# Strassen block products for the last four feed-forward blocks of an attention and gated feed-forward kernel, in a second pass of 768 tokens

## Chip, core and metric

One core of a Trainium2 chip runs the whole program. The metric is device time in microseconds, the median of several executions. Times inside an execution are from the hardware profiler: us from the first instruction.

## The reference

Eight batches of eight heads, 576 tokens, head size 64. Attention is linear: queries and keys are projected to 128 features, shifted by their largest magnitude, and taken through exp of plus and minus. The result goes through a gated feed-forward layer of 4608 tokens, model size 512, inner size 1536:

```python
def _moe_ref(x, w_gate, w_val, w_out):
    gate = 1.0 / (1.0 + np.exp(-(x @ w_gate)))
    val = x @ w_val
    return (gate * val @ w_out).astype(np.float32)
# x: attention output, (4608, 512); w_gate, w_val: (512, 1536); w_out: (1536, 512)
```

All inputs and outputs are float32.

## The kernel before

*The feed-forward layer.* Tokens are cut into 9 chunks of 512 (`CW`, `NCH`), the inner size into 12 blocks of 128 (`NJ`), the model size into 4 slices of 128. x lies feature-major: a tile is 128 features x 512 tokens. To keep float32 accuracy with one-pass matmuls, each operand is kept as two `float32r` halves, high (`xh`, `wh`, `hh`) and low (`xl`, `wl`, `hl`), and a product is three matmuls: high by high, high by low, low by high. For a chunk and a block, `gate` runs 4 slices x 3 matmuls for the gate and as many for the value, each with its own 128x128 weights and 512 moving columns. ScalarE takes tanh and exp of the gate; VectorE clears a sign bit, makes two combined steps with the value, and after ScalarE's rounding (`hh`) subtracts to get `hl`. `mm_out` multiplies the halves by the output weights: 3 matmuls of 512 columns for each of 4 token tiles.

*Stages.* While attention runs, `first_js` takes blocks 0 to 3 of every chunk whose x is ready, and stores half sums in `yscr`. After attention its memory is given to the second stage (`swap`): for each chunk C, blocks 4 to 11 (`js`) accumulate in four PSUM banks, and VectorE adds the stored y and sends the result out. Weights of blocks 4 to 7 lie in `vh`, `vl`, those of 8 to 11 take the place of blocks 0 to 3 in `wh`, `wl`. Each chunk's x is loaded twice for this stage: `zh`, `zl` for blocks 4 to 7, `xh`, `xl` for 8 to 11. `weigh` unpacks one 512-column weight piece of the float64-like input words into its halves.

*Order.* The program is not run as written. Each step is put into a plan (`pe`, `dve`, `on_act`, `sp`) with an assumed duration, a rank, and the buffers it reads and writes. `Plan.run` then lays all steps out: at each engine it starts, among steps that could start about first, the one of lowest rank. A step that needs a buffer of a ring takes the slot that is free earliest. Each engine runs its steps in that fixed order; semaphores do the waiting. The assumed cost of a VectorE step is 0.07 us plus 1/960 us an element, of a ScalarE step 0.08 plus 1/1200.

*PSUM.* Five banks are the ring `r_a` (named bank in the profile), three are `r_g` (gate).

Of the kernel before, what the change touches and what calls it, by code (L numbers as in the profile page):

```python
# [8 lines left out]
F32 = mybir.dt.float32  # L9
# [24 lines left out]
JA = 4  # L34
JR = 8
NQ = 3
# [9 lines left out]
XN = 4  # L46
HN = 5
FSTEP = 4.5
KOFF = 20.0
NOFF = 40.0  # L50


class Slot:
    def __init__(self, make):
        self.make, self.made, self.free, self.taken = make, None, 0.0, False

    def tile(self):
        if self.made is None:
            self.made = self.make()
        return self.made  # L60


class Buf:
# [6 lines left out]
    def __call__(self):  # L70
        if self.ap is None:
            x, n = self.slot.tile(), 1
# [20 lines left out]
class Plan:  # L93
# [29 lines left out]
    def run(self):  # L123
# [7 lines left out]
        def pick(b, taken):  # L131
            best = None
            for ring in b.rings:
                for s in ring:
                    if not s.taken and s not in taken and (best is None or s.free < best.free):
                        best = s
            return best

        def start(o):
            t = max(o.ready, free[o.eng])  # L140
            if o.eng == "PE" and mode not in (None, o.mode[0]):
                t = max(o.ready, free[o.eng] + self.SWITCH)
            taken = []
            for b in o.bufs:
                if b.rings and b.slot is None:
                    s = pick(b, taken)
                    if s is None:
                        return None
                    taken.append(s)
                    t = max(t, s.free)  # L150
            return t

        order, left = [], len(self.ops)
        while left:
# [19 lines left out]
            for b in o.bufs:  # L174
                if b.rings and b.slot is None:
                    b.slot = pick(b, ())
                    b.slot.taken = True
            free[o.eng] = t + o.busy
# [5 lines left out]
            if o.eng == "PE":  # L184
                mode = o.mode[-1]
            for slot in o.opens:
                slot.free, slot.taken = end, False
            for b in o.bufs:
                b.left -= 1
                b.end = max(b.end, end)  # L190
                if not b.left and b.slot:
                    b.slot.free, b.slot.taken = b.end, False
            for n in o.then:
# [14 lines left out]
def attention_moe(  # L208
# [21 lines left out]
    def ring(where, tag, n, width, dtype=F32):  # L230
        def make(i):
            pool = stage[where] if isinstance(where, str) else where
            return pool.tile([P, width], dtype, tag=f"{tag}{i}", name=f"{tag}{i}")

        return [Slot(lambda i=i: make(i)) for i in range(n)]

# [15 lines left out]
    xscr = [dram.tile([P, NC4, CW], F32, tag=f"xs{c}", name=f"xs{c}") for c in range(NCH)]  # L252
    yscr = [dram.tile([4, P, DM], F32, tag=f"ys{c}", name=f"ys{c}") for c in range(NCH)]
    dens = [dram.tile([2, S], F32, tag=f"den{i}", name=f"den{i}") for i in range(B * NP)]

    r_a = ring(ps, "bank", BANKS, DM)
    r_g = ring(ps, "gate", 8 - BANKS, DM)
    r_wh, r_wl = (ring(ff, f"w{a}", JA, 3 * DM, F32R) for a in "hl")
    r_xh, r_xl = (ring(ff, f"x{a}", XN, CW, F32R) for a in "hl")
    r_hh, r_hl = (ring(ff, f"h{a}", HN, CW, F32R) for a in "hl")  # L260
    r_u, r_t = (ring(ff, a, 2, CW) for a in "ut")
    r_y = ring(ff, "y", 2, DM)
    r_raw = ring(ff, "wraw", 2, 2 * DM, U32)
    r_mid = ring(ff, "wmid", 2, 2 * DM, U32) if RAW < 3 * JA else []
    r_top = ring(ff, "wtop", 2, DM, U32)
    r_wh2, r_wl2 = (ring("two", f"v{a}", JR - JA, 3 * DM, F32R) for a in "hl")
    r_xh2, r_xl2 = (ring("two", f"z{a}", NC4, CW, F32R) for a in "hl")
    r_hh2, r_hl2 = (ring("two", f"k{a}", 3, CW, F32R) for a in "hl")
    r_y1 = ring("two", "y1", 4, DM)
    at_rings = {}  # L270
# [13 lines left out]

    def dve(n, fn, reads, writes, rank, k=1.0):
        return plan.op("DVE", 0.07 + n / 960 / k, 0.16, fn, reads, writes, rank)

# [18 lines left out]
    ymark = [Buf() for _ in range(NCH)]  # L306
    closing = []

# [370 lines left out]

    def weigh(j, m, r, deep, rings):  # L680
        if m == 0:
            weights[j] = [(Buf([rings[0]], [P, 3 * DM]), Buf([rings[1]], [P, 3 * DM])), []]
        (wh, wl), _ = weights[j]
        ms = slice(m * DM, m * DM + DM)
        raw = Buf([r_raw], [P, 2 * DM])
# [5 lines left out]
        def hi():  # L691
# [3 lines left out]
            512 << 10,  # L695
            lambda: nc.sync.dma_start(raw(), w_moe[j, :, m, :].bitcast(U32)), [], [raw], r,
        )
        dve(
# [8 lines left out]
        if deep:  # L707
# [24 lines left out]
        on_act(  # L732
            DM, lambda: act.copy(wh()[:, ms], top().bitcast(F32)), [top], [(wh, m)], r,
        )
# [9 lines left out]
        else:  # L744
# [29 lines left out]
            ),  # L774
            [src], [(wl, m)], r,
        )

    def load_x(c, r, rings, after=()):
# [109 lines left out]
    for i in range(N):  # L888
        since = len(plan.ops)
        attend(i)  # L890
        closing += plan.ops[since:]
        if i < 4:
            for m in range(3):
                weigh(i, m, WAT + WSTEP * (3 * i + m), 3 * i + m >= RAW, (r_wh, r_wl))
        if i % NP == NP - 1:
            lo = 0 if i < NP else ((i // NP) * S) // CW
            for c in range(lo, ((i // NP + 1) * S) // CW):
                r = due(i + 1) + LEAD + 66.0 * (c - lo)
                if c:
                    load_x(c, r - 20.0, [(r_xh, r_xl)])  # L900
                first_js(c, r, FSTEP)

    def swap():
# [3 lines left out]
    last = plan.op("X", 0.0, 0.0, swap, after=closing)  # L907
    last.opens = [s for r in (r_wh2, r_wl2, r_xh2, r_xl2, r_hh2, r_hl2, r_y1) for s in r]
    for s in last.opens:
        s.taken = True  # L910

    base = due(N) + 60.0
    for j in range(JA, NJ):
        rings = (r_wh2, r_wl2) if j < JR else (r_wh, r_wl)
        for m in range(3):
            weigh(j, m, base + 10.0 * (j - JA) + 3 * m, False, rings)

    late = None
    js = list(range(JA, NJ))
    accs = {}  # L920
    for C in range(NCH):
        load_x(NCH + C, base + 150.0 + 100.0 * C, [(r_xh2, r_xl2)], [last])
        load_x(2 * NCH + C, base + 200.0 + 100.0 * C, [(r_xh, r_xl)], [last])
        for i, j in enumerate(js):
            r = base + 200.0 + 100.0 * C + 10.0 * i
            near = j < JR
            hs = gate(
                NCH + C if near else 2 * NCH + C, j, r, [r_g, r_a], False,
                (r_hh2, r_hl2) if near else (r_hh, r_hl),
            )  # L930

            def step(C=C, i=i, j=j, hs=hs, r=r):
                if i == 0:
                    accs[C] = [Buf([r_a], [P, DM]) for _ in range(4)]
                for t in range(4):
                    acc = accs[C][t]
                    pe(
                        "f", 0.685,
                        lambda acc=acc, t=t: mm_out(acc, t, hs, j, i == 0, i == len(js) - 1),
                        [*hs] + [(x, 2) for x in weights[j][0]], [acc], r + 13.0, 0.3,  # L940
                    )
                    if i == len(js) - 1:
                        y1, y = Buf([r_y1], [P, DM]), Buf([r_y], [P, DM])
                        sp(
                            256 << 10,
                            lambda t=t, y1=y1: nc.sync.dma_start(y1(), yscr[C][t]),
                            [(ymark[C], t)], [y1], r - 20.0, [last],
                        )
                        dve(
                            DM,  # L950
                            lambda y=y, y1=y1, acc=acc: vec.scalar_tensor_tensor(
                                y(), acc(), 0.5, y1(), op0=ALU.mult, op1=ALU.add
                            ),
                            [acc, y1], [y], -90.0,
                        )
                        sp(
                            256 << 10,
                            lambda t=t, y=y: nc.sync.dma_start(
                                out[C * CW + t * P : C * CW + t * P + P, :], y()
                            ),  # L960
                            [y], [], r,
                        )

            step()
    order = plan.run()
# [60 lines left out]
```

## Time and profile before

| | before |
|---|---|
| median of 3 executions | 1203.58 us (1202.52 to 1206.42) |
| the profiled execution | 1204.94 us, span 1203.0 us |
| TensorE (PE) busy | 1185.0 us, 99% |
| weight loads (PEld) | 914.8 us |
| VectorE (DVE) busy | 778.1 us |
| ScalarE (ACT) busy | 556.4 us |
| bytes moved by DMA | 129.04 MB |

A row of a group of instructions reads: source line, engine, operation, written tile <- read tiles, shapes, how many; then busy time and mean duration in ns, then idle time of the engine just before them and what ended it. A row of the timeline reads: start in us, length in us, engine, line, operation. A weight load is a LDWEIGHTS of engine PEld; it stands beside the matmuls of PE. L809 is the gate and value matmul, L857 the output matmul, L951 the final sum, L438 and L333 are projections of attention.

### The profile page before, as it was taken

To read this page: it belongs to the slowest core of one execution; us is meant where nothing else is said; L and a number is where in the kernel's file an instruction comes from. 1 tells how busy PE (TensorE), PEld (TensorE's weight loads), DVE (VectorE), ACT (ScalarE), POOL (GpSimd) and SP (SyncE) were. 2 spreads that over 40 slices of the span, in tenths; PEclk is the share of its full clock that TensorE was granted. 3 is DMA by queue.
4 is the path that set the end of the run, shared out by engine and by line. 5 is a ranking of instruction groups with operands and counts; after the bars stand their busy time and mean duration, and the time that the engine had idled before them with its cause. 6 is when DMAs were issued, how large, how long until landed. Compare 5 with 4: busy or idle time off the path is not lost.

```text
span 1203.0 us, 21037 instructions
## 1 busy us (share of the span) xinstructions
PE 1185.0 (99%) x8508; PEld 914.8 (76%) x8508; DVE 778.1 (65%) x1489; ACT 556.4 (46%) x1054; POOL 0.7 (0%) x6
## 2 busy tenths in 40 slices
PE   8999999999999999999999999999999999999998
PEld 6666567667776767778888888888888888888886
DVE  6999998887888888579849744344343444343433
ACT  6867776566666575545545422222222222222211
POOL 0000000000000000000000000000000000000000
PEclk9999999999999999999999999999999999999999
DMA  6763552534434441355334413121130213131300
GB/s 229 224 212 116 167 175 88 165 115 137 119 125 133 118 156 53 100 178 164 108 106 140 140 36 105 35 81 61 35 106 24 84 33 105 36 105 36 102 4 35
DMA packets 72936, 129.04 MB, mean 107 GB/s; under 512 B 16904, under 2 KB 23176, under 8 KB 72840
## 3 DMA queue, kind: packets, MB, share of 16 engines
q1 hardware_dynamic: 72840, 127.71, 33.5%
q8 instruction: 66, 1.08, 0.4%
q14 instruction: 30, 0.25, 0.1%
HBM read 99.09 MB, written 28.45 MB: 106 GB/s over the span
## 4 chain that ended last, share of the span: by engine, by line
PE 86%; DVE 6%; DMA 5%; ACT 1%; issue 1%; SPq 0%; DVEq 0%
PE gate L809 35%; PE bank L857 18%; PE bank L809 11%; PE gate L857 6%; PE bank L522 4%; PE bank L564 3%; PE bank L333 2%; DMA rb<-den 2%; PE bank L582 2%; PE bank L438 1%; DMA den<-dn 1%; PE bank L536 1%; PE bank L548 1%; DVE d L488 1%; DMA wraw<-w_moe 1%
## 5 line engine op out<-in xcount | busy, mean ns | idle before, releaser
L809 PE MATMUL gate<-xh,wh 128*128 128x512 f32 x464 | 183.5, 396 | 0.6 <-ACT u L829 0.6
L809 PE MATMUL gate<-xl,wh 128*128 128x512 f32 x464 | 180.9, 390 | 0.6 <-DVE xl L662 0.6
L809 PE MATMUL gate<-xh,wl 128*128 128x512 f32 x464 | 180.9, 390 | 0.0
L833 DVE TENSOR_SCALAR t<-t 128x512 uint32<-128x512 uint32 x108 | 45.6, 423 | 171.4 <-ACT t L828 171.3
L828 ACT ACTIVATE t<-gate 128x512 f32<-128x512 f32 x99 | 59.0, 596 | 189.0 <-PE gate L809 188.8
L846 ACT CAST hh<-u 128x512 fp32r<-128x512 f32 x72 | 44.7, 621 | 166.1 <-DVE u L843 166.0
L380 ACT ACTIVATE ek<-ek 128x512 f32<-128x512 f32 (+1 forms) x192 | 96.6, 526 | 28.4 <-DVE ek L368 27.1
L809 PEld LDWEIGHTS gate<-xh,wh 128*128 128x128 f32 x464 | 87.1, 188 | 20.4 <-issue 1.2
L809 PEld LDWEIGHTS gate<-xh,wl 128*128 128x128 f32 x464 | 87.1, 188 | 18.8
L809 PEld LDWEIGHTS gate<-xl,wh 128*128 128x128 f32 x464 | 87.2, 188 | 18.5 <-DVE xl L662 1.0
L809 PE MATMUL gate<-zl,vh 128*128 128x512 f32 x208 | 81.0, 389 | 0.0
L809 PE MATMUL gate<-zh,vl 128*128 128x512 f32 x208 | 81.0, 389 | 0.0
L809 PE MATMUL gate<-zh,vh 128*128 128x512 f32 x208 | 80.9, 389 | 0.0
L838 DVE SCALAR_TENSOR_TENSOR t<-t,gate 128x512 f32<-128x512 f32 x69 | 47.3, 685 | 51.9 <-PE gate L809 51.3
L843 DVE SCALAR_TENSOR_TENSOR u<-u,t 128x512 f32<-128x512 f32 x108 | 74.5, 690 | 7.6 <-DVE t L838 0.5
L522 PE MATMUL bank<-ek,vin 128*32 128x256 f32 x1240 | 73.3, 381 | 4.9 <-ACT d L446 4.0
L846 ACT CAST kh<-u 128x512 fp32r<-128x512 f32 x36 | 22.4, 621 | 117.6 <-DVE u L843 117.6
L522 PEld LDWEIGHTS bank<-ek,vin 128*32 128x32 f32 x1240 | 37.7, 110 | 46.0 <-issue 11.0
L848 DVE TENSOR_TENSOR hl<-u,hh 128x512 fp32r<-128x512 f32 x72 | 49.6, 689 | 30.9 <-ACT hh L846 30.9
L857 PE MATMUL bank<-wh,hl 128*128 128x512 f32 x168 | 65.6, 390 | 0.0
L857 PE MATMUL bank<-wh,hh 128*128 128x512 f32 x168 | 65.6, 390 | 0.0
L857 PE MATMUL bank<-wl,hh 128*128 128x512 f32 x168 | 65.3, 389 | 0.0
(176 smaller groups left out, 2475.5 us busy)
## 6 DMA issues: line engine op xcount, KB each, us to landing
wraw<-w_moe SPq DMA_DIRECT2D x36, 512.0 KB
xl<-xs SPq DMA_DIRECT2D x68, 256.0 KB
kin<-k SPq DMA_DIRECT2D x32, 320.0 KB
qin<-q SPq DMA_DIRECT2D x32, 320.0 KB
vin<-v SPq DMA_DIRECT2D x32, 320.0 KB
ys<-y SPq DMA_DIRECT2D x36, 256.0 KB
zl<-xs SPq DMA_DIRECT2D x36, 256.0 KB
y<-ys SPq DMA_DIRECT2D x36, 256.0 KB
```

The lines of the kernel that those rows point to most:

```text
L333: nc.tensor.matmul(pk[hd]()[:, t, :], x()[head(hd), t * P : t * P + P], wk[head(hd), :], start=True, stop=True,)
L380: lambda g=g, sg=sg: act.activation(ek[g]()[:, :, sg * F : sg * F + F], ek[g]()[:, :, F:], AF.Exp, scale=1.0 - 2.0 * sg,),
L522: nc.tensor.matmul(o_[o : o + Q, : 2 * F], vx()[:, 2 * t + hd, o % D : o % D + Q], (e0, e1)[hd][:, t, :] if t < 4 else e2[:, 0, :], start= ...
L564: nc.tensor.matmul(nm()[o : o + Q, :], w()[:, sg, o : o + Q], es[sg]()[:, o // D, cs], start=sg == 0, stop=sg == 1, tile_position=(0, o),)
L809: nc.tensor.matmul(o(), a()[:, ws], x(), start=cc + n == 0, stop=cc == NC4 - 1 and n == 2,)
L828: on_act(CW, lambda: act.activation(t(), g(), AF.Tanh, scale=0.5), [g], [t], z)
L833: vec.tensor_scalar(tu, tu, 0x7FFFFFFF, None, op0=ALU.bitwise_and)
L838: lambda: vec.scalar_tensor_tensor(t(), t(), 1.0, vl(), op0=ALU.add, op1=ALU.mult),
L843: lambda: vec.scalar_tensor_tensor(u(), u(), 1.0, t(), op0=ALU.min, op1=ALU.mult),
L846: on_act(CW, lambda: act.copy(hh(), u()), [u], [hh], z)
L848: CW, lambda: vec.tensor_tensor(hl(), u(), hh().bitcast(F32), op=ALU.subtract),
L857: nc.tensor.matmul(acc(), a()[:, ts], w()[:, ws], start=first and i == 0, stop=last and i == 2)
```

## The change

Blocks 8 to 11 leave the second stage and are done in a pass of their own after it. The second stage (pass 1 below) now takes blocks 4 to 7 alone (`JB = 8`) and stores its sums in `y2scr`. Pass 2 goes over 6 blocks of 768 tokens (`DC`), each two halves of 384 (`HT`). A pair of inner blocks by the model size's two halves makes a 2 by 2 grid of weight blocks, 256 x 128 each; x makes a 2 by 2 grid of 256 features x 384 tokens. Their product is made of seven block products in place of eight (Winograd's form of Strassen's scheme). One block product is 2 slices x 3 matmuls of 384 columns.

- `combine` builds, for each of 2 pairs and for gate and value, the seven weight operands in halves, in pass 1; `keep_out` stages the output weights in memory (`wscr`).
- `x_blocks` loads x for one block of tokens, makes T1 to T4 with four subtractions and splits seven operands.
- `group` runs the seven products in four PSUM banks of `r_a`. Three banks are written twice; VectorE adds in between and after.
- `gated` and `valued` are the former gate steps in pieces of 384. Output parts accumulate in `r_g`; `finish` adds the stored sum and sends it out.
- All rings of the feed-forward layer become ranges of a few large tiles (`arena`), so that the passes can use the same memory differently; a slot is free when all of its cells are. `turn` opens pass 2's loads once pass 1's loads and staged weights are through.

The core of the diff, and the new functions:

```diff
-    base = due(N) + 60.0
-    for j in range(JA, NJ):
-        rings = (r_wh2, r_wl2) if j < JR else (r_wh, r_wl)
...
+    for j in range(JA, JB):
+        weigh_all(j, base + 10.0 * (j - JA), 3, lambda m: False, (r_wh2, r_wl2))
...
+    def combine(n, m, r):
...
+        for i in range(2):
+            weigh(JB + 2 * n + i, m, r + 3 * i, False, gh, gl, ...)
+            dve(DM, ...)       # w = gh + gl
+        for o, a, b, op, reads in (
+            (0, (w, 2), (w, 3), ALU.add, [(w, 1)]),
+            (1, (x, 0), (w, 0), ALU.subtract, [(w, 0)]),
+            (2, (w, 1), (x, 1), ALU.subtract, [(w, 0)]),
+            (3, (w, 0), (w, 2), ALU.subtract, [w]),
+        ):
+            dve(KH, ...)
+        for n_, o, i in ((3, 4, 0), (1, 2, 3)):
+            on_act(n_ * KH, ...)   # high halves
+            dve(n_ * KH, ...)      # low halves
...
+    js = list(range(JA, JB))
+    for C in range(NCH):
+        load_x(NCH + C, r0 - 20.0, [(r_zh2, r_zl2) if C > 1 else (r_zh, r_zl)], ...)
...
+    turn = plan.op("X", 0.0, 0.0, lambda: None, after=loads + staged)
...
+    def x_blocks(dc, r):
...
+        fetch(b11, 0, 0)
+        fetch(tmp[0], 0, 1)
+        fetch(b22, 1, 1)
+        fetch(b21, 1, 0)
+        less(tmp[1], tmp[0], b11)
+        split("11", b11)
+        less(tmp[2], b22, tmp[1])
+        split("T2", tmp[2])
+        less(tmp[0], b22, tmp[0])
+        split("T3", tmp[0])
+        split("T1", tmp[1])
+        less(tmp[2], b21, tmp[2])
+        split("21", b21)
+        split("T4", tmp[2])
+        split("22", b22)
...
+    def group(n, m, x, r):
+        gh, gl = blocks[n, m]
+        a, b, c, d = (Buf([r_a], [P, CW]) for _ in range(4))
+        t1, t2, t3 = (Buf([r_f], [P, HT]) for _ in range(3))
...
+                for cc in range(2):
+                    for i_, (s, y) in enumerate(((gh, xh), (gh, xl), (gl, xh))):
+                        nc.tensor.matmul(o()[:, :HT], s()[:, ws], y()[:, cc, :], ...)
...
+        product(a, 0, "11", "11", True, False)
+        on_act(HT, lambda: act.copy(t1(), a()[:, :HT]), [a], [t1], -200.0)
+        product(b, 1, "S2", "T2", True, True)
+        add(t1, t1, b)
+        product(c, 2, "S3", "T3", True, False)
+        add(t2, t1, c)
+        product(d, 3, "S1", "T1", True, False)
+        add(t2, t2, d)
+        product(a, 4, "12", "21", False, True)
+        product(c, 5, "22", "T4", False, True)
+        add(t3, t1, c)
+        product(d, 6, "S4", "22", False, True)
+        add(t1, t1, d)
+        return a, t2, t3, t1
...
+    for dc in range(NDC):
+        r = base2 + 46.0 * dc
+        x = x_blocks(dc, r - 20.0)
+        for n in range(NB):
+            gg = group(n, 0, x, r + 14.6 * n)
+            ut = gated(n, gg, hs[n])
+            vv = group(n, 1, x, r + 14.6 * n + 7.3)
+            valued(ut, vv, hs[n])
+        for T in range(DC // P):
+            for n in range(NB):
+                pe("f", 1.37, out_part, ..., r + 29.2 + 1.4 * T + 0.7 * n, 0.3)
+            finish(dc * (DC // P) + T, acc, y2scr, y2mark, ...)
```

More of the change, by code (lines that the diff above doesn't have):

```diff
@@ L34 @@
 JA = 4
-JR = 8
+JB = 8
+HT = 384
+DC = 2 * HT
+NDC = NT // DC
+CELL = 64
+RA = 86 << 10
+RB = 84 << 10
+FB = 3 << 10
+NQ4 = JB - JA
 NQ = 3
@@ L50, with __init__, at, take @@
 NOFF = 40.0
+HSTEP = 2.0
+class Cells:
+    def __init__(self, n):
+        self.free, self.taken = [0.0] * n, [False] * n
 class Slot:
[L54 to L60, printed above, removed]
+    def __init__(self, cells, first, n, view):
+        self.cells, self.first, self.last, self.view = cells, first, first + n, view
+    def at(self):
+        c = self.cells
+        if any(c.taken[self.first : self.last]):
+            return None
+        return max(c.free[self.first : self.last])
+    def take(self):
+        n = self.last - self.first
+        self.cells.taken[self.first : self.last] = [True] * n
+    def give(self, t):
+        n = self.last - self.first
+        self.cells.taken[self.first : self.last] = [False] * n
+        self.cells.free[self.first : self.last] = [t] * n
+    def hits(self, other):
+        return (
+            self.cells is other.cells
+            and self.first < other.last
+            and other.first < self.last
+        )
+class Area:
+    def __init__(self, tile, cells, start=0):
+        self.tile, self.cells, self.next = tile, cells, start
+    def ring(self, n, width, dtype=None):
+        out = []
+        for _ in range(n):
+            size = -(-width * 4 // CELL)
+            o = self.next * CELL // 4
+            def view(o=o):
+                x = self.tile()[:, o : o + width]
+                return x if dtype is None else x.bitcast(dtype)
+            out.append(Slot(self.cells, self.next, size, view))
+            self.next += size
+            assert self.next <= len(self.cells.free), (self.next, len(self.cells.free))
+        return out
 class Buf:
@@ L71, in __call__ @@
         if self.ap is None:
[L72 removed]
+            x, n = self.slot.view(), 1
             if self.dtype is not None:
@@ L149, in start @@
                     taken.append(s)
-                    t = max(t, s.free)
+                    t = max(t, s.at())
             return t
@@ L176, in run @@
                     b.slot = pick(b, ())
-                    b.slot.taken = True
+                    b.slot.take()
             free[o.eng] = t + o.busy
@@ L185, in run @@
                 mode = o.mode[-1]
-            for slot in o.opens:
-                slot.free, slot.taken = end, False
+            for cells in o.opens:
+                n = len(cells.free)
+                cells.free, cells.taken = [end] * n, [False] * n
             for b in o.bufs:
@@ L191, in run @@
                 if not b.left and b.slot:
-                    b.slot.free, b.slot.taken = b.end, False
+                    b.slot.give(b.end)
             for n in o.then:
@@ L230, in ring, with view, arena @@
     def ring(where, tag, n, width, dtype=F32):
[L231 to L235, printed above, removed]
+        cells, made = Cells(n), {}
+        def view(i):
+            if i not in made:
+                pool = stage[where] if isinstance(where, str) else where
+                made[i] = pool.tile([P, width], dtype, tag=f"{tag}{i}", name=f"{tag}{i}")
+            return made[i]
+        return [Slot(cells, i, 1, lambda i=i: view(i)) for i in range(n)]
+    def arena(where, name, size, dtype):
+        made = []
+        def view():
+            if not made:
+                pool = stage[where] if isinstance(where, str) else where
+                made.append(pool.tile([P, size // 4], dtype, tag=name, name=name))
+            return made[0]
+        cells = Cells(size // CELL)
+        return lambda start=0: Area(view, cells, start * 1024 // CELL)
     ebias = const.tile([P, 1], F32, name="ebias")
@@ L257, in attention_moe @@
     r_g = ring(ps, "gate", 8 - BANKS, DM)
[L258 to L269, printed above, removed]
+    low, high = arena(ff, "low", RA, F32R), arena("two", "high", RB, F32R)
+    flat, more = arena(ff, "flat", 32 << 10, F32), arena("two", "more", FB, F32)
+    x = low()
+    r_wh, r_wl = (x.ring(JA, 3 * DM) for _ in range(2))
+    r_xh, r_xl = (x.ring(XN, CW) for _ in range(2))
+    r_hh, r_hl = (x.ring(HN, CW) for _ in range(2))
+    x = flat()
+    r_u, r_t = (x.ring(2, CW) for _ in range(2))
+    r_y = x.ring(2, DM)
+    r_raw, r_mid = (x.ring(2, 2 * DM, U32) for _ in range(2))
+    r_top = x.ring(2, DM, U32)
+    x = high()
+    r_w2 = x.ring(2 * NQ4, 3 * DM)
+    r_wh2, r_wl2 = r_w2[::2], r_w2[1::2]
+    r_zh, r_zl = x.ring(6, CW), x.ring(6, CW)
+    r_k = x.ring(6, CW)
+    x = low(56)
+    r_zh2, r_zl2 = r_zh + x.ring(2, CW), r_zl + x.ring(2, CW)
+    r_y1 = x.ring(4, DM)
+    r_wst = x.ring(7, DM)
+    r_G = low().ring(8, 7 * 2 * P)
+    r_X = low(56).ring(10, 2 * HT)
+    x = high()
+    r_X += x.ring(4, 2 * HT)
+    r_h = x.ring(8, 2 * HT)
+    r_y1b = x.ring(4, DM)
+    r_wo = high(48).ring(8, DM)
+    r_f = flat().ring(5, HT)
+    x = flat(12)
+    r_tmp = x.ring(3, 2 * HT)
+    r_f += x.ring(7, HT) + more().ring(FB // (4 * HT), HT)
     at_rings = {}
@@ L678, in attend, with weigh @@
             t += wd
[L680 to L684, printed above, removed]
+    def weigh(j, m, r, deep, wh, wl, ms, part, after=()):
         raw = Buf([r_raw], [P, 2 * DM])
@@ L696, in weigh @@
             lambda: nc.sync.dma_start(raw(), w_moe[j, :, m, :].bitcast(U32)), [], [raw], r,
+            after,
         )
@@ L774, in weigh, with weigh_all @@
             ),
-            [src], [(wl, m)], r,
+            [src], [(wl, part)], r,
         )
+    def weigh_all(j, r, step, deep, rings):
+        wh, wl = Buf([rings[0]], [P, 3 * DM]), Buf([rings[1]], [P, 3 * DM])
+        weights[j] = [(wh, wl), []]
+        for m in range(3):
+            weigh(j, m, r + step * m, deep(m), wh, wl, slice(m * DM, m * DM + DM), m)
     def load_x(c, r, rings, after=()):
@@ new lines, in attention_moe @@
+    last.opens = [a().cells for a in (high, more)]
+    for cells in last.opens:
+        cells.taken = [True] * len(cells.free)
+    fed = plan.op("X", 0.0, 0.0, lambda: None, after=feeding)
+    done = plan.op("X", 0.0, 0.0, lambda: None, after=opening)
+    base = due(N) + 60.0
+    for j in range(JA, JB):
+        weigh_all(j, base + 10.0 * (j - JA), 3, lambda m: False, (r_wh2, r_wl2))
+    blocks, wo, combined = {}, {}, []
+    names = ["11", "12", "S3", "22", "S1", "S2", "S4"]
+    KH = 2 * P
@@ new lines, in attention_moe, with keep_out @@
+    wmark = {}
+    def keep_out(j, r):
+        wh, wl = Buf([r_wst], [P, DM]), Buf([r_wst], [P, DM])
+        weigh(j, 2, r, False, wh, wl, slice(0, DM), None, [done])
+        for n, x in enumerate((wh, wl)):
+            wmark[j, n] = Buf()
+            staged.append(sp(
+                256 << 10,
+                lambda n=n, x=x: nc.sync.dma_start(wscr[j - JB][n], x().bitcast(F32)),
+                [x], [wmark[j, n]], r,
+            ))
+    staged = []
+    for n in range((NJ - JB) // 2):
+        for m in range(2):
+            combine(n, m, base + 210.0 + 36.0 * n + 12.0 * m)
+        for i in range(2):
+            keep_out(JB + 2 * n + i, base + 234.0 + 36.0 * n + 4 * i)
@@ new lines, in attention_moe @@
+    js = list(range(JA, JB))
+    span = 33.0
+    y2mark = [Buf() for _ in range(NCH)]
+    loads = []
+    for C in range(NCH):
+        r0 = base + 200.0 + span * C
+        since = len(plan.ops)
+        load_x(NCH + C, r0 - 20.0, [(r_zh2, r_zl2) if C > 1 else (r_zh, r_zl)], [last] + [fed] * (C > 1))
+        loads += plan.ops[since:]
+        accs = []
+        for i, j in enumerate(js):
+            r = r0 + 8.2 * i
+            hs = gate(NCH + C, j, r, [r_g, r_a], False, (r_k, r_k))
+            if i == 0:
+                accs = [Buf([r_a], [P, DM]) for _ in range(4)]
+            for t in range(4):
+                acc = accs[t]
+                pe(
+                    "f", 0.685,
+                    lambda acc=acc, t=t, hs=hs, j=j, i=i: mm_out(
+                        acc, t, hs, j, i == 0, i == len(js) - 1
+                    ),
+                    [*hs] + [(x, 2) for x in weights[j][0]], [acc], r + 13.0, 0.3,
+                )
+                if i == len(js) - 1:
+                    got = finish(
+                        4 * C + t, acc, yscr, ymark, lambda c, t: y2scr[c][t],
+                        lambda c, t: [(y2mark[c], t)], [r_mid] if C < 2 else [r_y1] if C < NCH - 1 else [r_wst], r,
+                        [] if C < 2 else [done] if C < NCH - 1 else staged,
+                    )
+                    loads.append(got)
@@ new lines, in attention_moe, with rank, fetch, less @@
+    turn = plan.op("X", 0.0, 0.0, lambda: None, after=loads + staged)
+    base2 = base + 200.0 + span * NCH
+    for j in range(JB, NJ):
+        wo[j] = Buf([r_wo], [P, DM]), Buf([r_wo], [P, DM])
+        for n in range(2):
+            sp(
+                256 << 10,
+                lambda x=wo[j][n], j=j, n=n: nc.sync.dma_start(
+                    x().bitcast(F32), wscr[j - JB][n]
+                ),
+                [wmark[j, n]], [wo[j][n]], base2 - 10.0, [turn],
+            )
+    def x_blocks(dc, r):
+        at_ = {n: (Buf([r_X], [P, 2, HT]), Buf([r_X], [P, 2, HT])) for n in XB}
+        tmp = [Buf([r_tmp], [P, 2, HT]) for _ in range(3)]
+        n_, since = [0.0], len(plan.ops)
+        def rank():
+            n_[0] += 0.1
+            return r + n_[0]
+        def fetch(x, K, h):
+            t, e = dc * DC + h * HT, dc * DC + h * HT + HT
+            s = 0
+            while t < e:
+                c, o = divmod(t, CW)
+                wd = min(CW - o, e - t)
+                sp(
+                    wd << 10,
+                    lambda c=c, o=o, s=s, wd=wd: nc.sync.dma_start(
+                        x().bitcast(F32)[:, :, s : s + wd],
+                        xscr[c][:, 2 * K : 2 * K + 2, o : o + wd],
+                    ),
+                    [xmark[c]], [x], rank(), prior[-1:],
+                )
+                t, s = t + wd, s + wd
+        def less(o, a, b):
+            dve(
+                2 * HT,
+                lambda: vec.tensor_tensor(
+                    o(), a().bitcast(F32), b().bitcast(F32), op=ALU.subtract
+                ),
+                [x for x in (a, b) if x is not o], [o], rank(),
+            )
+        def split(n, src):
+            xh, xl = at_[n]
+            on_act(
+                2 * HT, lambda: act.copy(xh(), src().bitcast(F32)), [src], [xh], rank()
+            )
+            dve(
+                2 * HT,
+                lambda: vec.tensor_tensor(
+                    xl(), src().bitcast(F32), xh().bitcast(F32), op=ALU.subtract
+                ),
+                [src, xh] if src is not xl else [xh], [xl], rank(),
+            )
+        b11, b21, b22 = (at_[n][1] for n in ("11", "21", "22"))
+        fetch(b11, 0, 0)
[13 more added lines that the diff above has]
+        split("22", b22)
+        prior.append(plan.op("X", 0.0, 0.0, lambda: None, after=plan.ops[since:]))
+        return at_
@@ new lines, in attention_moe, with product, go, add @@
+    prior = [turn]
+    XB = ("11", "T2", "T3", "T1", "21", "T4", "22")
+    taken = [turn]
+    def group(n, m, x, r):
+        gh, gl = blocks[n, m]
+        a, b, c, d = (Buf([r_a], [P, CW]) for _ in range(4))
+        t1, t2, t3 = (Buf([r_f], [P, HT]) for _ in range(3))
+        def product(o, i, w, xn, first, last):
+            k, (xh, xl) = names.index(w) * KH, x[xn]
+            def go():
+                for cc in range(2):
+                    ws = slice(k + cc * P, k + cc * P + P)
+                    for i_, (s, y) in enumerate(((gh, xh), (gh, xl), (gl, xh))):
+                        nc.tensor.matmul(
+                            o()[:, :HT], s()[:, ws], y()[:, cc, :],
+                            start=first and cc + i_ == 0, stop=cc + i_ == 3,
+                            skip_group_check=not first,
+                        )
+            o_ = pe("f", 1.05, go, [gh, gl, xh, xl], [o], r + 1.04 * i, 0.3, taken[-1:])
+            if first:
+                taken.append(o_)
+        def add(o, p, q):
+            dve(
+                HT,
+                lambda: vec.tensor_tensor(o(), p(), q()[:, :HT], op=ALU.add),
+                [y for y in (p, q) if y is not o], [o], -200.0,
+            )
+        product(a, 0, "11", "11", True, False)
[12 more added lines that the diff above has]
+        return a, t2, t3, t1
```

202 lines of the change are left out of this document (147 added, 55 removed).

## The prediction

> **What bounds the kernel now.** I read the busy line of the page first, then the chain of waits, then busy time by stretch, then the waits of the engines, then the groups of instructions with shapes kept apart.
>
> ```profile
> PE 1185.0 (99%) x8508; PEld 914.8 (76%) x8508; DVE 778.1 (65%) x1489; ACT 556.4 (46%) x1054; POOL 0.7 (0%) x6
> PE 86%; DVE 6%; DMA 5%; ACT 1%; issue 1%; SPq 0%; DVEq 0%
> 100.00:200.00 100.00, 96.50 (x1290) 63.84 (x1291) 91.09 (x196) 76.23 (x150) 0.00 (x0) 1.00 0.50 153
> 300.00:400.00 100.00, 100.00 (x1046) 70.33 (x1038) 84.04 (x175) 62.98 (x125) 0.00 (x0) 1.00 0.43 128
> 600.00:1195.00 595.00, 595.00 (x2620) 491.55 (x2619) 271.84 (x452) 173.89 (x309) 0.00 (x0) 1.00 0.22 69
> PE bank L333 <- DMA kin<-k: 4.5, 1, 4.5
> L809 PE MATMUL gate<-xh,wh 128*128 128x512 f32 x464 | 183.5, 396 | 0.6 <-ACT u L829 0.6
> L809 PEld LDWEIGHTS gate<-xh,wh 128*128 128x128 f32 x464 | 87.1, 188 | 20.4 <-issue 1.2
> ```
>
> TensorE is the bound. A busy matmul row proves little by itself, since pipelined matmuls overlap; the stretch row (columns: stretch, its length, PE busy and count, PEld, DVE, ACT, POOL, clock, DMA share, GB/s) says more: from 600 to 1195 us, 2620 matmuls of 512 columns start in 595 us, one every 0.2271 us, at full granted clock, while DVE is busy 46% and ACT 29%. Nothing stands between the matmuls there, so time goes down only with fewer or shorter matmuls, as long as the other engines keep up. The longest wait of TensorE in the whole run is 4.5 us, at the start.
>
> **The change, part by part.**
>
> *Gate and value matmuls of blocks 8 to 11.* Removed: 9 chunks x 4 blocks x 24 = 864 matmuls of 512 columns, at 0.2271 us: 196.2 us. Added: 6 token blocks x 2 block pairs x 2 (gate, value) x 7 products x 6 = 1008 matmuls of 384 columns. The output matmuls stay 432 of 512 columns. No row has an f32r matmul of 384 columns; its step is the largest term and comes from these rows (duration min/median/max; start, length; the last two are runs of eight):
>
> ```profile
> L333 PE MATMUL bank<-wk,kin x496: 269/272/579, 4.5 to 482.0; 64*128 64x128 f32 x166
> L438 PE MATMUL bank<-qin,wk x116: 589/590/693, 33.6 to 482.6; 64*128 64x512 f32 x116
> 304.88 0.19 PEld L857 LDWEIGHTS gate<-wh,hh 128*128 128x128 f32 x1
> 304.91 0.49 PE L857 MATMUL gate<-wh,hh 128*128 128x512 f32 x1
> 304.99 0.19 PEld L857 LDWEIGHTS gate<-wl,hh 128*128 128x128 f32 x1
> 305.23 0.39 PE L857 MATMUL gate<-wl,hh 128*128 128x512 f32 x1
> 13.15 0.97 PEld L407 LDWEIGHTS gate<-minus,mq 128*128 128x128 f32 x8
> 13.26 1.06 PE L407 MATMUL gate<-minus,mq 128*128 128x128 f32 x8
> ```
>
> The attention's plain f32 matmul grows from 272 to 590 ns between 128 and 512 columns, 0.828 ns a column, so 512 columns are 424 ns of it. The f32r matmul of 512 columns lasts 0.39 us, 200 ns less, so its columns cost (424 - 200) / 512 = 0.437 ns, and 128 columns fewer save 56 ns: 0.2271 - 0.056 = 0.171. If the step shrinks in proportion, it is 0.1703; at half the f32 cost a column (0.414), 0.1741. I take 0.1715, nearest to the row of the same type: 1008 x 0.1715 = 172.9, a saving of 23.3 us (20.7 to 24.5).
>
> This supposes that a weight load hides under 0.17 us of matmul. Its recorded 188 ns is longer than that. But eight loads of 128x128 in a row stand in 0.97 us: (0.97 - 0.19) / 7 = 0.111 us each, with matmuls every (1.06 - 0.275) / 7 = 0.112 beside them; and the load at 304.99 comes 0.11 after the one before. So a load occupies its path 0.11 us, the rest is latency. I cost loads at nothing; what covers them is the matmul before, with 0.06 us to spare.
>
> *Pass 1 (blocks 4 to 7).* Its matmuls are the same count. Its chunk ends, where four accumulators wait for DVE and four y loads, come every 144 x 0.2271 = 32.7 us in place of 65; the stretch from 600 to 1195 holds several such ends at PE 100%, so I cost them at 0. Weight preparation stays 36 pieces. Building the S blocks adds per pair and matrix about 4.3 us of DVE (two 512-, four 256-, one 768- and one 256-element step), 17 us over some 290 us in which DVE has half its time free; 0 on the path. Nine chunks x 4 more y results out and back, and the four blocks' output weights out and back, are added on SP's queue; one issue is shown below at 0.60 us, and the DMA engines are 22% busy. 0; were that cover gone, one late y load holds an accumulator a few us.
>
> *Pass 2, DVE and ACT.* Durations by shape, then three independent DVE steps in a row:
>
> ```profile
> L368 DVE TENSOR_TENSOR ek<-bank,mk 128x128 f32<-128x128 f32 x30 | 8.5, 284 | 0.6 <-ACT d L451 0.2
> L793 DVE TENSOR_TENSOR xl<-xl,xh 128x512 fp32r<-128x512 f32 x68 | 44.4, 682 | 0.2 <-ACT xh L788 0.2
> L488 DVE TENSOR_TENSOR d<-d,mb 128x1152 f32<-128x1152 f32 x29 | 39.1, 1347 | 0.0
> L833 DVE TENSOR_SCALAR t<-t 128x512 uint32<-128x512 uint32 x108 | 45.6, 423 | 171.4 <-ACT t L828 171.3
> L571 ACT COPY ex<-bank 128x288 f32<-128x288 f32 x60 | 23.5, 395 | 5.9 <-PE bank L564 5.7
> L846 ACT CAST hh<-u 128x512 fp32r<-128x512 f32 x72 | 44.7, 621 | 166.1 <-DVE u L843 166.0
> L491 ACT ACTIVATE eq<-d 128x1152 f32<-128x1152 f32 x29 | 33.8, 1167 | 24.3 <-DVE d L488 24.2
> 648.05 0.69 DVE L793 TENSOR_TENSOR zl<-zl,zh 128x512 fp32r<-128x512 f32 x1
> 648.65 0.69 DVE L727 SCALAR_TENSOR_TENSOR wtop<-wraw,wtop 128x512 uint32<-128x512 uint32 x1
> 649.26 0.69 DVE L793 TENSOR_TENSOR zl<-zl,zh 128x512 fp32r<-128x512 f32 x1
> 305.17 0.60 SPq L623 DMA_DIRECT2D dn<-dr  x1
> ```
>
> Between 128 and 1152 elements a DVE step grows 1.04 ns an element: 0.55 us for 384, 0.95 for 768; the bit mask 0.34. In a row they start 0.60 apart for a recorded 0.69, so 0.085 of each is overlap. One block of 768 tokens has on DVE: x blocks 4 + 7 steps of 768 (10.4 us), 20 additions of 384 (11.0), 8 masks (2.7), 24 gate-value steps (13.2), 6 final sums (4.1): 41.4 us as recorded, 35.6 by start-to-start (less 69 x 0.085). ACT: 7 casts of 768 (some 0.85), 4 copies, 16 activations, 8 casts of 384 (some 0.5): 20 us. TensorE's own time for the block: 168 x 0.1715 + 72 x 0.2271 = 45.2 us. So DVE goes from 46% to 92% busy, and becomes the engine to watch. Between the two stretches quoted, DVE at 84% cost TensorE nothing, and at 91% it stood beside 3.5% idle (not all DVE's). Bounds for six blocks, 271 us: 0 and 9.5 us. I take 3, nearer to the first, since by start-to-start DVE is 79% full.
>
> Two places matter in a block. Inside a group of seven products (1.03 us each) banks c and d are read by DVE and then written again. How fast that goes, the last gate chain shows:
>
> ```profile
> 1191.87 0.39 PE L809 MATMUL bank<-xh,wl 128*128 128x512 f32 x1
> 1192.29 0.69 DVE L838 SCALAR_TENSOR_TENSOR t<-t,bank 128x512 f32<-128x512 f32 x1 [1.66 <-PE bank L809]
> 1193.08 0.69 DVE L843 SCALAR_TENSOR_TENSOR u<-u,t 128x512 f32<-128x512 f32 x1
> 1193.81 0.62 ACT L846 CAST hh<-u 128x512 fp32r<-128x512 f32 x1 [3.15 <-DVE u L843]
> 1194.46 0.69 DVE L848 TENSOR_TENSOR hl<-u,hh 128x512 fp32r<-128x512 f32 x1 [0.69 <-ACT hh L846]
> 1195.20 0.19 PEld L857 LDWEIGHTS bank<-wh,hl 128*128 128x128 f32 x1 [0.20 <-DVE hl L848]
> 1197.38 0.39 PE L857 MATMUL bank<-wh,hl 128*128 128x512 f32 x1
> 1195.74 1.39 DVE L951 SCALAR_TENSOR_TENSOR y<-bank,y 128x512 f32<-128x512 f32 x2 [0.59 <-PE bank L857]
> 1198.65 1.39 DVE L951 SCALAR_TENSOR_TENSOR y<-bank,y 128x512 f32<-128x512 f32 x2 [1.52 <-DMA out<-y]
> ```
>
> DVE starts 0.03 after a matmul's end, 0.19 after its slot. Bank d's first product ends its slot 4.1 us into the group, its addition is done at 4.9, and the product that writes d again starts at 6.2: 1.2 us to spare, one long step of the x blocks (0.95) but not two. At the block's end, the last value's chain takes some 2.4 us by the same rows scaled to 384, plus two additions; three output parts of the other pair (3 x 6 x 0.2271 = 4.1 us) stand in three banks ahead of it. That fits with about 0.5 to spare. The next block's x is made meanwhile: from the last group's start to the next block 23.7 us, with some 21 us of DVE work by start-to-start. Late next would be its products T3 and on.
>
> *The turn between the passes.* The first x blocks must be fetched, subtracted and split in memory that pass 1 still uses; by my count 8 to 11 of 14 buffers come free before pass 1 ends, so the last three or four splits come late. Between 0 (all ready) and one unhidden fetch and split, 4.5 (the kernel's first wait) + 0.62 + 0.68 = 5.8. I take 2, since "11" and T2, which come first, have their buffers.
>
> *The end.* Now the last matmul ends at 1197.8 and the span at 1203.0: two of four sums wait 1.5 us for a y buffer. In pass 2 the sums come 2.7 us apart, so the tail is 0.2 + 0.7 + the 3.0 us from the last sum's end (1200.0) to 1203.0, 3.9 us: 1.3 less (0 to 1.5).
>
> *Sum* against the profiled execution's 1204.94 us: - 23.3 - 1.3 + 2 + 3 = 1185.3. The median of the runs is 1.4 below that execution: 1184.
>
> **Rivals.**
>
> *DVE short in pass 2, chance 0.12.* The upper bounds come true: 9.5 and 5.8 us. For it: 92% busy as recorded. Against: 79% by starts. 1204.9 - 24.6 + 15.3 - 1.4 = 1194 us; 1190 to 1200 with it.
>
> *The loads show, 0.06.* If a load's whole 188 ns must fit under the matmul before, the step is 0.189: a saving of 5.7 us, 1204.9 - 5.7 - 1.3 + 5 - 1.4 = 1201.5, no change. Against it: loads 0.11 apart. The Trainium skill, TensorE: Matmul & The Clock Gate, Part 3, "What overlaps and what doesn't", would have it worse: a load overlaps a running matmul only where the row groups differ, and here all loads take all rows. By that page's times (columns / 1.2 for a load, columns / 2.4 for a matmul) the estimate is 864 x 0.320 - 1008 x 0.267 = 7 us saved. The trace disagrees at 512 columns: the load at 304.99 lies inside the matmul at 304.91.
>
> *Returns to a bank hold TensorE, slower, 0.11.* In each of the 24 groups the products that write c and d again wait for DVE. It decides from (24.6 - 2) / 24 = 0.94 us a group. If DVE is two long x steps behind and one more 384 step (2 x 0.95 + 0.55 - 1.2 = 1.25 us late), it costs 30 us: 1204.9 - 24.6 + 2 + 30 - 1.4 = 1211 us. For it: DVE takes its work in order, and x steps stand between the additions. Against: while the groups run, additions, masks and the first pair's value steps fill DVE only some 17 of 28.8 us by starts, and most x steps fall beside the output parts.
>
> **How the numbers follow.** Forecast 0.71 (1178 to 1191), DVE short 0.12, loads 0.06, returns 0.11. A measurement of this kernel tells 0.3%, 3.6 us, from no change. Faster is the forecast and DVE short, with a little of the loads case: 0.84; same 0.05; slower 0.11. The range starts where all bounds help, 1204.9 - 24.5 - 1.5 - 1.4 = 1177.5, and ends at 1200, which takes in DVE short and leaves out loads and returns, 0.17.
>
> **What would show it.** Matmuls of 384 columns start 0.170 to 0.174 us apart: the main term is right; 0.189: the loads. Pass 2's stretches show PE at 97% or more, DVE near 90%; waits of PE on DVE additions at c and d, in sum over 20 us, mean the returns. Waits on x casts or splits once, of 0 to 6 us, are the turn; at each block, DVE short. After the last matmul some 4 us remain. The forecast is wrong if waits in pass 2 exceed 4 us a block.

## The result, and the profile after

The changed kernel takes 1184.48 us (median of 4, 1183.81 to 1185.86), the kernel before 1204.78 on the same chips; the ratio is 0.9834, interval 0.9813 to 0.9855. Run twice more beside other kernels it gave 0.9840 both times (0.9827 to 0.9853 and 0.9815 to 0.9865). The forecast was 1184, faster. The ratio is clear of 1 and 1.7% below it.

The page of the profiled execution (1183.81 us, span 1182.0):

```profile
PE 1166.2 (99%) x8652; PEld 928.0 (79%) x8652; DVE 904.0 (76%) x1755; ACT 591.4 (50%) x1128; POOL 0.7 (0%) x6
```

TensorE has 144 matmuls more and is 18.8 us less busy. The next row is the busy time in pass 2 (stretch, length, PE, PEld, DVE, ACT, POOL, clock, DMA share, GB/s). Below it stands all that TensorE waited for from 900 us on, which is one row (waiting engine, who ended the wait; us in total, times, longest):

```profile
951.00:1178.00 227.00, 227.00 (x1196) 212.88 (x1194) 178.80 (x334) 87.43 (x168) 0.00 (x0) 1.00 0.32 96
PE bank L1247 <- DVE low L1204: 0.4, 1, 0.4
```

From 951 us on TensorE works without a gap, and DVE is busy 178.8 of 227 us, 79%. The step, the time from one matmul's start to the next one's, is read from the first and last start of one block's products (L1247; 128 + 40 = 168 matmuls) and from a block's 72 output matmuls in a row:

```profile
L1247 PE MATMUL bank<-low x128: 333/335/343, 1041.4 to 1069.5; 128*128 128x384 f32 x128
L1247 PE MATMUL bank<-high,low x40: 330/333/338, 1042.6 to 1070.5; 128*128 128x384 f32 x40
933.76 16.49 PE L1354 MATMUL gate<-high 128*128 128x512 f32 x72
```

(1070.5 - 1041.4) / 167 = 0.174 us at 384 columns; (16.49 - 0.39) / 71 = 0.2268 at 512, where 0.39 is the last one's own length. Read in the trace to the nanosecond the first is 0.1741. At 384 the loads nearly fill PEld (212.9 of 227 us), and still nothing waits for them.

The span fell by 21.0 us. The step accounts for 196.2 - 1008 x 0.1741 = 20.7; the end, 5.2 to 3.7 us, for 1.5; and pass 2 lost some 0.8 us, nearly all in its first block. The rest, 0.4 us of the other sign, is within what two executions differ by (1183.81 to 1185.86).

### The profile page after: what moved, and what is told of

It is laid out like the page before. It is cut to its first block, busy times and chain, and to the rows that moved or that the text cites. A ratio compares the mean times of both kernels' runs of the same rounds, so it can differ in the third digit from the quotient of the medians.

```text
span 1182.0 us, 21892 instructions
## 1 busy us (share of the span) xinstructions
PE 1166.2 (99%) x8652; PEld 928.0 (79%) x8652; DVE 904.0 (76%) x1755; ACT 591.4 (50%) x1128; POOL 0.7 (0%) x6
## 4 chain that ended last, share of the span: by engine, by line
PE 83%; DVE 8%; DMA 5%; ACT 2%; issue 1%; SPq 0%; DVEq 0%
PE gate L909 22%; PE bank L1247 14%; PE bank L957 9%; PE gate L1354 8%; PE bank L909 7%; PE gate L957 6%; PE bank L618 4%; PE bank L660 3%; DMA rb<-den 2%; PE bank L429 2%; PE bank L678 2%; DMA den<-dn 1%; PE bank L534 1%; DVE d L584 1%; PE bank L632 1%
## 5 line engine op out<-in xcount | busy, mean ns | idle before, releaser
L909 PE MATMUL gate<-low 128*128 128x512 f32 x744 | 177.0, 394 | 1.2 <-ACT flat L929 0.6
L909 PEld LDWEIGHTS gate<-low 128*128 128x128 f32 x744 | 137.7, 188 | 31.6 <-issue 1.2
L1247 PE MATMUL bank<-low 128*128 128x384 f32 x728 | 151.9, 337 | 0.4 <-DVE low L1204 0.4
L1247 PEld LDWEIGHTS bank<-low 128*128 128x128 f32 x728 | 129.0, 188 | 1.2 <-DVE low L1204 0.7
L909 PE MATMUL gate<-high 128*128 128x512 f32 x468 | 113.6, 390 | 0.0
L957 PE MATMUL bank<-high 128*128 128x512 f32 x432 | 105.1, 392 | 0.2 <-DVE high L948 0.2
L909 PEld LDWEIGHTS gate<-high 128*128 128x128 f32 x468 | 87.9, 188 | 18.7
L1354 PE MATMUL gate<-high 128*128 128x512 f32 x432 | 99.1, 390 | 0.0
L957 PEld LDWEIGHTS bank<-high 128*128 128x128 f32 x432 | 81.0, 188 | 18.2 <-DVE high L948 0.6
L1354 PEld LDWEIGHTS gate<-high 128*128 128x128 f32 x432 | 81.1, 188 | 16.5
L957 PE MATMUL gate<-low 128*128 128x512 f32 x384 | 92.8, 395 | 0.0
L938 DVE SCALAR_TENSOR_TENSOR flat<-flat,gate 128x512 f32<-128x512 f32 x66 | 45.2, 685 | 57.8 <-PE gate L909 57.2
L957 PEld LDWEIGHTS gate<-low 128*128 128x128 f32 x384 | 70.9, 188 | 15.4 <-issue 1.0
L1247 PE MATMUL bank<-high,low 128*128 128x384 f32 x280 | 72.3, 335 | 0.0
L1260 DVE TENSOR_TENSOR flat<-flat,bank 128x384 f32<-128x384 f32 x98 | 54.0, 551 | 20.2 <-PE bank L1247 19.5
```

Source lines behind the costliest of these rows:

```text
L909: nc.tensor.matmul(o(), a()[:, ws], x(), start=cc + n == 0, stop=cc == NC4 - 1 and n == 2,)
L938: lambda: vec.scalar_tensor_tensor(t(), t(), 1.0, vl(), op0=ALU.add, op1=ALU.mult),
L957: nc.tensor.matmul(acc(), a()[:, ts], w()[:, ws], start=first and i == 0, stop=last and i == 2)
L1247: nc.tensor.matmul(o()[:, :HT], s()[:, ws], y()[:, cc, :], start=first and cc + i_ == 0, stop=cc + i_ == 3, skip_group_check=not first,)
L1260: lambda: vec.tensor_tensor(o(), p(), q()[:, :HT], op=ALU.add),
L1354: nc.tensor.matmul(acc(), s()[:, h, o : o + P], w(), start=n + i + k_ == 0, stop=n == NB - 1 and i == 1 and k_ == 2,)
```

## The experiments

**Eight products in the second pass.** The usual products, no S and no T:

```diff
-        product(a, 0, "11", "11", True, False)
-        on_act(HT, lambda: act.copy(t1(), a()[:, :HT]), [a], [t1], -200.0)
-        product(b, 1, "S2", "T2", True, True)
...
+        product(a, 0, "11", "11", True, False)
+        product(a, 1, "12", "21", False, True)
+        product(c, 2, "21", "11", True, False)
+        product(c, 3, "22", "21", False, True)
+        product(b, 4, "11", "12", True, False)
+        product(b, 5, "12", "22", False, True)
+        product(d, 6, "21", "12", True, False)
+        product(d, 7, "22", "22", False, True)
```

> The second pass with the same tiles of 768 tokens, but each 2 by 2 grid from the usual eight block products: no S, no T, no additions by VectorE. Theory (the gain is the eighth product): TensorE spends 6 x (192 x 0.1741 + 72 x 0.2268) = 298.5 us on pass 2 in place of 273.4, so 1184.5 + 25 = 1209.6 us, slightly slower than before, since a matmul of 384 columns also carries a fixed cost. Rival (the gain comes from the second pass itself: other tiles, less x traffic per matmul, a shorter end): it stays at 1185 to 1192 us.

Measured: 1208.65 us against 1206.24 of before on that chip, ratio 1.0024 (1.0013 to 1.0035). One block, 160 + 32 = 192 matmuls, and the stretch of its pass 2:

```profile
L1201 PE MATMUL bank<-low x160: 333/334/346, 1056.5 to 1089.7; 128*128 128x384 f32 x160
L1201 PE MATMUL bank<-high,low x32: 331/335/338, 1061.8 to 1089.8; 128*128 128x384 f32 x32
957.00:1200.00 243.00, 243.00 (x1294) 229.92 (x1293) 108.27 (x202) 66.16 (x134) 0.00 (x0) 1.00 0.25 80
```

The step is the same, (1089.8 - 1056.5) / 191 = 0.174, with DVE at 45% in place of 79%. So the second pass by itself gains nothing; it loses a little, as shorter matmuls cost more a column (0.1741 / 384 against 0.2268 / 512). The whole gain is the eighth product. In the traces the way from the first product's start to the last output matmul's takes 301.7 us (904.3 to 1206.0) in place of 277.0 (901.0 to 1178.0): 24.7 more, against 25 worked out. By the ratios it is 1.0024 - 0.984, some 22 us of 1205; the difference of 2 to 3 us is a little over what the two intervals allow, and isn't explained.

**Halves of 256, and of 128.** These change one size (`HT`; the plan's ranks and assumed length of a product are scaled with it) and ask what a matmul costs that is shorter still:

```diff
-HT = 384
+HT = 256
```

> Pass 2 in blocks of 512 tokens, halves of 256: 1512 matmuls of 256 columns in place of 1008 of 384, still seven products. Theory (a slot is 13.8 ns and 0.4167 ns a column, weight loads hidden at 0.111 us each): slot 0.1205 us, pass 2 takes 9 x (168 x 0.1205 + 48 x 0.2268) = 280.2 us against 273.4, so 1191.3 us. Rival 1 (a load's recorded 188 ns must fit under the matmul before): slot 0.19, 1296 us. Rival 2 (the slot is proportional to the columns): slot 0.113, 1181 us.

> Pass 2 in blocks of 256 tokens, halves of 128: 3024 matmuls of 128 columns, each with its own weight load. Theory (a load occupies its path 0.111 us and hides only under matmuls longer than that): slot 0.112 us in place of the 0.066 that columns and the fixed part give, pass 2 takes 18 x (168 x 0.112 + 24 x 0.227) = 437 us against 273, so 1348 us. Rival 1 (the recorded 188 ns of a load bind): 18 x (168 x 0.19 + 5.4) = 672, 1583 us. Rival 2 (loads never bind): 18 x (168 x 0.066 + 5.4) = 297, 1208 us.

Measured: 1190.2 us (before 1206.24; ratio 0.9864, 0.9847 to 0.9880) for 256, and 1346.74, a single execution, for 128 (before 1205.0). One block of each:

```profile
L1247 PE MATMUL bank<-low x136: 274/282/283, 1031.5 to 1051.2; 128*128 128x256 f32 x136
L1247 PEld LDWEIGHTS bank<-low x128: 188/192/192, 1050.4 to 1069.0; 128*128 128x128 f32 x128
L1247 PE MATMUL bank<-high,low x40: 223/276/276, 1050.4 to 1068.9; 128*128 128x128 f32 x40
```

The first row is of 256 (the block's other 32 matmuls lie between its ends), the others of 128. The step is (1051.2 - 1031.5) / 167 = 0.118, and (1068.9 - 1050.4) / 167 = 0.111. From 512 to 384 to 256 columns it goes 0.2268, 0.1741, 0.118. That is 0.41 ns a column over the first 128 and 0.44 over the next, which leaves between 0.006 and 0.016 us that each matmul pays whatever its width. Carried on to 128 columns, those two slopes give 0.062 to 0.069, and the step is 0.111, as eight loads in a row had it before: there a load of 128x128 sets it. Its recorded 188 to 192 ns set it in none of these runs. The times lie 1.1 and 1.3 us from the theory, and 106 and 236 us below what 188 ns would give. For 256 that nearness is partly luck: against before the loss to the changed kernel is 0.9864 - 0.984, 2.9 us, where the theory has 6.8, since its step of 0.1205 was too long.

**More work for VectorE.** 16 or 28 steps more in a block, each right behind a product; this is the form with 28, the other has `if i < 4` in place of `if True`:

```diff
             if first:
                 taken.append(o_)
+            if True:
+                dve(
+                    HT,
+                    lambda: vec.tensor_reduce(
+                        junk, ident.unsqueeze(1).broadcast_to([P, 3, P]), axis=AX.X, op=ALU.max
+                    ),
+                    [], [], -200.0, after=[o_],
+                )
```

> As the changed kernel, with 16 more VectorE steps of 384 elements in each block of 768 tokens (four in each group of seven products, right behind a product; they read a constant and nobody reads them). Counted by start-to-start (0.47 us each) VectorE has 35.6 + 7.5 = 43.1 us of work in 45.6: no loss, 1184 to 1190 us. Counted by recorded durations (0.55 each) it has 41.4 + 8.8 = 50.2: 4.6 us over in each of six blocks, 1212 us.

> The same with 28 more steps in each block (one behind each of the 28 products). By start-to-start VectorE has 35.6 + 13.2 = 48.8 us in 45.6: it becomes the bound, 3.2 us over in each of six blocks, 1204 us. By recorded durations 56.8 us: 1252 us. If VectorE had much more room than either count says, 1185 us.

Measured: 1187.96 us, ratio 0.9852 (0.9837 to 0.9866), and 1211.43 us, ratio 1.0045 (1.0030 to 1.0059), both beside 1206.24. Pass 2 of the two, then what TensorE waited for longest in the second, and a short stretch of it:

```profile
952.00:1180.00 228.00, 227.88 (x1196) 213.27 (x1196) 211.31 (x415) 87.76 (x168) 0.00 (x0) 1.00 0.31 96
952.00:1200.00 248.00, 237.78 (x1199) 214.87 (x1198) 242.33 (x483) 91.41 (x171) 0.00 (x0) 0.99 0.28 90
PE gate L1364 <- ACT high L1332: 8.0, 5, 2.2
1045.70:1049.00 3.30, 3.30 (x9) 2.63 (x8) 3.30 (x6) 1.25 (x2) 0.00 (x0) 0.50 0.00 0
```

At 211 of 228 us, 93%, TensorE stands idle for 0.1 us of the stretch (227.88 of 228.00), and the run is some 1.5 us slower than the changed kernel (0.9852 against 0.984), within the intervals. At 242 of 248, 98%, DVE is the bound and costs some 24 us. The count by start-to-start told both apart: the first lies in its range, the second is 7 us above it. The count by recorded durations missed both, by 24 and 41 us. Where it gives way is mainly not the banks (1.0 us in one wait) but the block's end, where output parts (L1364) wait for the last value's halves.

Part of what the second lost beyond the count is clock. The last row has a granted clock of 0.50: from 1045.7 to 1049.0 the output matmuls start 0.427 us apart and not 0.2268, eight of them, 1.6 us. It happens twice in its pass 2, soon after a block end's waits, and costs some 3.4 us in all. The changed kernel's pass 2 has clock 1.00 throughout (its row above). That the waits bring it on was not tested.

**Returns to a bank at once.** The order of products, and a fixed sequence:

```diff
-            if first:
-                taken.append(o_)
+            taken.append(o_)
...
         product(c, 2, "S3", "T3", True, False)
         add(t2, t1, c)
-        product(d, 3, "S1", "T1", True, False)
-        add(t2, t2, d)
-        product(a, 4, "12", "21", False, True)
-        product(c, 5, "22", "T4", False, True)
+        product(c, 3, "22", "T4", False, True)
         add(t3, t1, c)
-        product(d, 6, "S4", "22", False, True)
+        product(d, 4, "S1", "T1", True, False)
+        add(t2, t2, d)
+        product(d, 5, "S4", "22", False, True)
         add(t1, t1, d)
+        product(a, 6, "12", "21", False, True)
```

> As the changed kernel, with the seven products of a group in a fixed order that returns to a bank at once: a, b, c, c again, d, d again, a again, none started before the one ahead of it. Theory (what hides VectorE's additions is the distance of two products before a bank is written again): each second product waits for the first one's end and one addition, 0.19 + 0.03 + 0.55 + 0.1 = 0.87 us, two of them in each of 24 groups: 24 x 1.74 = 42 us more, 1226 us. Rival (additions don't hold TensorE): 1184 to 1188 us.

Measured: 1234.95 us, a single execution; 1205.0 before. One return in the timeline of TensorE, and its waits from 906 us on:

```profile
1176.48 1.39 PE L1247 MATMUL bank<-low 128*128 128x384 f32 x7
1178.61 1.30 PE L1247 MATMUL bank<-low 128*128 128x384 f32 x6 [0.74 <-DVE flat L1259]
...
PE bank L1247 <- DVE flat L1259: 18.2, 26, 1.2
PE gate L1353 <- ACT high L1321: 13.6, 6, 2.8
PE bank L1247 <- DVE more L1259: 2.1, 3, 0.8
```

Each return that shows lost about 0.9 us from slot end to start (the matmul that begins at 1176.48 + 6 x 0.174 = 1177.53 ends its slot at 1177.70, the next starts at 1178.61), as worked out. But only 26 + 3 of 48 show: around the others the plan had output parts to put in. In exchange each block's end waits 1.4 to 2.8 us, since the last value now comes later, and twice the granted clock is 0.50 for some 3.4 us behind such a wait (1054.9 to 1058.2 is one), which is 2.8 us. Step by step, the trace has some 30 us lost inside the groups and 21 at the blocks' ends. So the total was nearly foreseen, 50 us (1234.95 - 1184.94, the changed kernel on the same chip) in place of 42, out of a sum that wasn't. The distance of two products is what keeps the changed kernel's additions free.

**Where pass 1's x lies.** In the changed kernel's pass 1 four of nine chunks run at 0.230 us a matmul, not 0.2267: those whose x halves lie partly in the low area, the large tile `low`, which has two of x's eight slots; the other six lie in `high`.

```diff
-        load_x(NCH + C, r0 - 20.0, [(r_zh2, r_zl2) if C > 1 else (r_zh, r_zl)], ...)
+        load_x(NCH + C, r0 - 20.0, [(r_zh, r_zl)], ...)
```

> As the changed kernel, but in pass 1 the x halves of all chunks use the six slots each in the high area; the two extra slots each in the low area are not used. In the changed kernel's trace the chunks of pass 1 that have x tiles in the low area (four of nine) run at 230 to 232 ns a matmul, the others at 227. Theory (where the operands lie costs it): all chunks at 227, 4 x 144 x 4 ns = 2.3 us less, 1182 us on the chip of the first comparison. Rival 1 (something else that alternates by chunk): no change. Rival 2 (eight slots are needed to have x ready): waits at the chunks' starts, a few us more.

Measured: 1195.02 us, ratio 0.9920 (0.9907 to 0.9932). Beside it the changed kernel itself, 1184.94:

> The changed kernel itself, beside z6 on the same chip: the same ratio to before as in the first comparison, 0.981 to 0.986; the 12 matmuls at the turn and the slots by chunk as in its first trace.

Late in pass 1, chunks that ran at 0.230 now run at 0.2267 (here 36 + 12 matmuls, 10.65 us in 47 steps), but early there are waits, where the changed kernel's TensorE was busy for all of 640 to 730 us:

```profile
L909 PE MATMUL gate<-high x36: 389/389/389, 816.8 to 827.5; 128*128 128x512 f32 x36
645.00:735.00 90.00, 82.62 (x352) 66.00 (x351) 78.91 (x153) 37.87 (x66) 0.00 (x0) 0.98 0.53 174
718.22 6.02 PE L909 MATMUL gate<-high 128*128 128x512 f32 x17 [4.21 <-DVE high L893]
```

Both theory and second rival hold, as far as this goes: without the low slots the slow steps, 3.5 ns a matmul, are gone, and with six slots x comes late while DVE is also unpacking weights. By the steps in the trace pass 1 gains some 2 us by the first and loses 11 by the second; of the 11 some 1.7 are again clock, 0.50 from 718.5 on (17 matmuls in 6.02 us, above). So a mixture was tried, the extra slots for chunks 2 and 3 only (`1 < C < 4`):

> As the changed kernel, but in pass 1 only the chunks C = 2 and 3 may use the two extra x slots in the low area; the others use six. With six for all, waits for x came at 636 to 730 us, in chunks 1 to 3, and every gate matmul ran at 0.2267 us. Theory (place of the operands costs, and eight slots are needed early only): chunks 4, 6 and 8 go from 0.230 to 0.227, 3 x 144 x 0.0037 = 1.6 us less, and no new wait: 1183 us where the changed kernel has 1184.7, a ratio to before of 0.983. Rival (six slots make x late in the later chunks too): 1186 us or more.

> The changed kernel beside zmix on the same chip: a ratio to before of 0.984.

Measured: 1185.44 us, ratio 0.9837 (0.9812 to 0.9862), beside 1185.07 of the changed kernel. Its chunks 4, 6 and 8 do run at 0.2267 and no new wait came, but 1.6 us is less than such a comparison tells. No version was found that is measurably faster than the changed kernel.

## Why the prediction was right, and where its terms were off

*The bound.* Right: TensorE before and after, and time fell with the number of products alone (eight products: 1.0024).

*The 384-column step.* The mechanism was right, the size off. Forecast 0.1715, measured 0.1741; forecast saving 23.3 us, measured 20.7, the low end of the range given. The failed step is the choice among three ways to take 128 columns off: 0.437 ns a column came out of two durations (390 and 590 ns) whose latencies were set equal. Between 512 and 384 columns the step shrank by 0.412 ns a column; half the f32 slope, 0.414, which was the other bound, was right there.

*The loads.* Right, and now shown: hidden at 384 and 256, the bound at 128, where one takes 0.111 us. The rule quoted from the Trainium skill, TensorE: Matmul & The Clock Gate, Part 3, "What overlaps and what doesn't", that a load overlaps a running matmul only with other row groups, doesn't hold in pass 2 of any run here: its loads take all rows, and 384 columns step at 0.174 us, not at a load plus a matmul.

*DVE in pass 2.* 3 us were set aside, and some 0.1 lost after the first block. The forecast took DVE to be 92% busy, by adding recorded durations, and set that beside busy shares of the page. Those shares count overlap once: the page says 79%, which is the start-to-start count (35.6 of 45.2). The comparison with the stretch at 91% was between unlike numbers, and the sign it gave for this, DVE near 90%, did not come. The runs with more DVE work show where the edge is: work of 43.1 us by start-to-start in a block of 45.6 costs under 2 us in the whole run, 48.8 some 24.

*Returns to a bank.* Right: no wait in the trace, and a return without the distance costs 0.9 us, 0.87 worked out in its experiment.

*The turn.* 2 us set aside, some 0.7 lost: the first block's products start in pieces among pass 1's last output matmuls, with one wait of 0.4 on a split.

*The end.* Forecast 3.9 us after the last matmul, measured 3.7 (matmul end 1178.4, span 1182.0).

*The sum.* 20.7 + 1.5 - 0.8 in place of 23.3 + 1.3 - 5: two misses of 2.6 and 4.2 us against each other. A third is the 1.4 us taken off because the profiled execution was slower than the median of three: with the fourth execution the median before is 1204.78, only 0.2 below it. That the point came within 0.5 us is luck. The range, not the point, was earned.

## What to carry to other kernels

When TensorE is packed, a scheme that takes out products pays what the product's matmuls cost, in steps measured at the new width, as long as the added vector work is hidden. Count that work by start-to-start times, because recorded durations overlap. Keep at least one addition's time, with its waits, between a product and the next write of its bank. Before cutting matmuls narrower, compare them with the weight load's step, not with its recorded length.

## What the hardware showed that was not expected

- A matmul's step went with where x was put: 0.230 to 0.2314 us with part of x in the low area, 0.2267 without, in the same places in all three traces of the changed kernel. The output matmuls of those chunks, which read no x, slow down too (0.2284 to 0.2309). So do some in the kernel before, which has no such area: 12 output matmuls at 0.230 from 1132.10 on, 0.2267 on either side. So place alone is not shown to be the cause, and it was not settled.
- DVE was 93% busy beside a TensorE that stood idle for 0.1 us of 228.
- In each of the three runs that made TensorE wait for more than 2 us at once late in the program, the granted clock was 0.50 for some 3.4 us at one or two places soon after, and matmuls of 512 columns started 0.427 us apart.
- A matmul of 128 columns with its own load costs nearly as much (0.111) as one of 256 (0.118).
